# Two batches taken jointly through three parallel matrices by seven half products, with other conversion steps and first loads ahead of a branch

## The chip, the cores and the metric

The kernel runs on one core of one Trainium2 chip. A core has five engines that matter here: TensorE (PE, the matrix products; PEld are its weight loads), VectorE (DVE), ScalarE (ACT), GpSimd (POOL) and SyncE (SP), which issues most DMAs. The metric is the time of one execution on the device, in microseconds (us); less is better. A kernel's time is the median over its runs.

## What is computed

Four batches of softcap attention (12 heads, 448 tokens, 64 wide) give 1792 tokens of 768 numbers. Two feed-forward parts follow, each token by itself:

```python
x = softcap_attention(q, k, v, cap)             # 4 x 448 tokens, 768 wide
h = x @ w_in                                    # 768 -> 2048
g = where(h >= 1, h, where(h <= -1, 0, (h + 1)**2 / 4))
x = g @ w_out                                   # 2048 -> 768
h = maximum(maximum(x @ w1, x @ w2), x @ w3)    # three parallel matrices, 768 -> 768
out = h @ w_out2                                # the last matrix, 768 -> 768
```

The weights are float64 in memory, everything else is fp32.

## The kernel before

**Layout and products.** Activations lie transposed, so a tile is 128 features by the 448 tokens of one batch. A product of a 128x128 piece of a weight with such a tile is called a **part**: both factors are divided into a high and a low half (hi, lo; type fp32r), and a part is three matmuls of 128x448, hi with hi, hi with lo and lo with hi (`parts`, L863, L864, L865). For one batch w_in takes 16 x 6 = 96 parts, w_out 96, the three parallel matrices (W123) 108, the last matrix (W2) 36.

**Conversion.** There are 64 weight units: 16 of w_in (128x768), 24 of w_out (128x512), 18 of W123 and 6 of W2 (128x768). `fetch_first` (L385) loads a unit's 64-bit words and makes fp32 of them in steps: `s0` (L405, on ACT at L408 or on DVE) scales the low word to a few bits, `sign` (L414, DVE, L415) copies the sign bit, `s1` (L420, ACT, L422) rescales the high word, `s3` (L424, DVE, L426) puts them together in a tile named wf; the result is stored in DRAM (`scratch`). For later batches `fetch_again` loads it from there. `weights` (L454) divides wf into its halves w: hi by a copy on ACT (L276) or DVE (L278), lo by a subtraction on DVE (L281). In batch 1 the halves that the last stage uses are also stored (`parted`).

**Stages.** Batch 0's attention comes first (11 to 70 us). The first six units of w_in are then used in plain fp32 (`PLAIN`, one matmul L858 for a part). Then come batch 0's layers, with batch 1's attention between them (to about 320 us), batch 1's layers with the attention of batches 2 and 3 (to about 613 us), and `last_two` (from 625 us to the end): batches 2 and 3 jointly through all four layers by `strassen` (L1041), which makes a 2x2 block product from seven half products instead of eight (L1263). There a stage is one half product for a group of three blocks, in six banks of PSUM; the four weight sums (tiles ss) and the operand sums (tiles op) come from DVE, and what PE leaves in a bank is taken out and added by ACT or DVE (`put`, `plus`, tiles named s, sc, sv, M, Y, O).

**Attention.** For a pair of heads: scores (ps_s, L578 or L589), tanh (L596, ACT), exp (L643, ACT), sums of the exponentials (`total`, ps_r, L672), their reciprocals and the product with v (ps_a, L798). For the reciprocals a row of sums rs (L728 on ACT, L730 on DVE) is turned over by DMAs: `gather` (L744, issued at L750 from ACT's queue, rs to rc) and `spread` (SP's queue). `ADDED` tells of each batch how many additions of exponential tiles DVE makes before PE sums the rest: with 3, PE has 8 short matmuls (112x224) for a pair; with 2, 16.

**Order.** Every operation is handed to the class `Plan` with a cost on each engine that may do it, a time at which it is wanted, and what it depends on. `Plan.run` places all of them in one fixed order for each engine and chooses the engine (ACT or DVE) of copies. Engines work their own lists in that order; a tile of a pool (u, h, w, wf, raw, and in PSUM s, a, m) is taken when its last user is done. Everything exists twice, in the two arms of a `tc.If` on the cap's bits; with the cap of 30 the second arm runs (keep_max False). The load of the cap's bits (L204) comes ahead of the branch, all other loads after it.

## Time and profile before

| | before |
|---|---|
| time, median of 3 runs | 996.36 us (995.25 to 998.95) |
| the profiled execution's own time | 995.53 us |
| its span in the trace | 993.7 us, so 1.83 us lie outside it |
| granted TensorE clock, mean over the span | 0.993 |
| busy: PE, DVE, ACT, POOL | 963.0, 748.0, 602.0, 0.2 us |

The busy times are those of the whole span: PE is busy 97% of it by the profile, with pipelined matmuls whose records overlap. So a window in which PE is shown as fully busy can still hold time in which it waited; what its instructions need is better taken from the pitch of a long run of them. The rows are in the section behind the change.

### The profile page before, as it was taken

The numbers are of one execution on the slowest core, as the hardware profiler recorded it, in microseconds if no ns is written. First come the engines' busy times: TensorE is split into PE (matmuls) and PEld (weight loads), VectorE is DVE, ScalarE is ACT, GpSimd is POOL, SyncE is SP. The second block draws the span as 40 slices with busy tenths as digits, with TensorE's granted clock in tenths as the row PEclk, the third lists the DMA queues.
The fourth block names the chain that finished last, engine by engine and source line by source line (L and its number), as shares of the span: only waits on it lengthen the run. The fifth ranks groups of instructions, "written<-read, shape, count | busy, mean of one in ns | idle before, by whom it ended". The sixth has DMA issues, their size and how long they took to land.

```text
span 993.7 us, 14604 instructions
## 1 busy us (share of the span) xinstructions
PE 963.0 (97%) x5356; PEld 769.6 (77%) x5356; DVE 748.0 (75%) x1205; ACT 602.0 (61%) x876; POOL 0.2 (0%) x4
## 2 busy tenths in 40 slices
PE   5799999999999999999999999999999999999998
PEld 1124777877868877777777778999999999999997
DVE  1679999998989677877655667676898767858782
ACT  4788999787888478754445555555764524232431
POOL 0000000000000000000000000000000000000000
PEclk9799999999999999999999999999999999999999
DMA  5448877898898878688898765572364347437243
GB/s 127 150 147 261 264 230 226 266 292 274 289 293 270 293 248 277 224 283 286 289 319 275 228 209 188 166 238 80 129 200 139 107 147 235 136 103 238 88 147 131
DMA packets 111533, 210.96 MB, mean 212 GB/s; under 512 B 13022, under 2 KB 71518, under 8 KB 111454
## 3 DMA queue, kind: packets, MB, share of 16 engines
q1 hardware_dynamic: 109930, 209.87, 66.3%
q8 instruction: 44, 0.72, 0.3%
q10 hardware_dynamic: 1524, 0.08, 0.1%
q14 instruction: 35, 0.29, 0.1%
HBM read 142.90 MB, written 66.93 MB: 211 GB/s over the span
## 4 chain that ended last, share of the span: by engine, by line
PE 77%; ACT 9%; DVE 7%; DMA 4%; issue 2%; ACTq 0%; SPq 0%; DVEq 0%
PE ps_m L1263 21%; PE ps_s L1263 11%; PE ps_m L863 9%; PE ps_m L865 8%; PE ps_m L864 8%; PE ps_a L798 6%; PE ps_a L1263 5%; PE ps_s L578 4%; ACT raw L408 3%; PE ps_m L858 3%; DVE raw L415 2%; ACT t L643 2%; ACT raw L422 1%; DVE wf L426 1%; PE ps_s L589 1%
## 5 line engine op out<-in xcount | busy, mean ns | idle before, releaser
L1263 PE MATMUL ps_m<-op,w 128*128 128x448 f32 x1008 | 212.2, 368 | 0.0
L1263 PEld LDWEIGHTS ps_m<-op,w 128*128 128x128 f32 x1008 | 189.2, 188 | 19.1
L281 DVE TENSOR_TENSOR w<-wf,w 128x768 fp32r<-128x768 f32 (+1 forms) x146 | 120.6, 828 | 9.8 <-ACT w L276 8.0
L596 ACT ACTIVATE t<-ps_s,qscale 112x896 f32<-112x896 f32 x96 | 92.5, 1002 | 45.8 <-PE ps_s L578 39.2
L1263 PE MATMUL ps_s<-op,w 128*128 128x448 f32 x522 | 112.2, 368 | 0.0
L1263 PEld LDWEIGHTS ps_s<-op,w 128*128 128x128 f32 x522 | 98.0, 188 | 9.9
L643 ACT ACTIVATE t<-t,cap_sb 112x896 f32<-112x896 f32 x96 | 96.0, 1039 | 4.8 <-DVE rs L730 3.0
L276 ACT ACTIVATE w<-wf 128x768 fp32r<-128x768 f32 (+1 forms) x86 | 64.4, 750 | 55.9 <-PE ps_m L865 34.3
L798 PE MATMUL ps_a<-t,v 112*32 112x448 f32 (+1 forms) x752 | 82.8, 564 | 3.0 <-DVE xf L281 1.5
L863 PE MATMUL ps_m<-y,w 128*128 128x448 f32 x216 | 80.6, 373 | 0.0
L865 PE MATMUL ps_m<-y,w 128*128 128x448 f32 x216 | 79.2, 367 | 0.8 <-DVE w L281 0.8
L864 PE MATMUL ps_m<-y,w 128*128 128x448 f32 x216 | 79.0, 366 | 0.0
L278 DVE CAST w<-wf 128x512 fp32r<-128x512 f32 (+1 forms) x60 | 29.5, 492 | 57.3 <-PE ps_m L865 44.2
L863 PE MATMUL ps_m<-g,w 128*128 128x448 f32 x192 | 71.8, 374 | 0.0
L865 PE MATMUL ps_m<-g,w 128*128 128x448 f32 x192 | 70.5, 367 | 1.4 <-DVE w L281 1.4
L864 PE MATMUL ps_m<-g,w 128*128 128x448 f32 x192 | 70.3, 366 | 0.0
L422 ACT ACTIVATE raw<-raw 128x768 f32<-128x768 f32 (+1 forms) x64 | 53.6, 839 | 27.5 <-DVE raw L415 22.9
L415 DVE TENSOR_SCALAR raw<-raw 128x768 uint16<-128x768 uint16 (+1 forms) x64 | 60.1, 938 | 11.8 <-ACT raw L408 10.8
L408 ACT ACTIVATE raw<-raw 128x768 uint16<-128x768 uint32 (+1 forms) x37 | 62.9, 1700 | 2.2 <-DMA raw<-in_w_out 1.0
L281 DVE TENSOR_TENSOR w<-ss,w 128x384 fp32r<-128x384 f32 x80 | 43.7, 555 | 24.9 <-ACT w L276 22.8
L798 PEld LDWEIGHTS ps_a<-t,v 112*32 112x32 f32 (+1 forms) x752 | 24.2, 114 | 48.6 <-issue 32.8
L276 ACT ACTIVATE w<-ss 128x384 fp32r<-128x384 f32 x69 | 35.3, 520 | 40.8 <-PE ps_m L1263 21.0
(140 smaller groups left out, 1730.4 us busy)
## 6 DMA issues: line engine op xcount, KB each, us to landing
p<-w SPq DMA_DIRECT2D x60, 384.0 KB
w<-p SPq DMA_DIRECT2D x60, 384.0 KB
w<-wf SPq DMA_DIRECT2D x40, 384.0 KB
wf<-w SPq DMA_DIRECT2D x40, 384.0 KB
wf<-w SPq DMA_DIRECT2D x80, 192.0 KB
raw<-in_w SPq DMA_DIRECT2D x18, 768.0 KB
raw<-in_w_in SPq DMA_DIRECT2D x16, 768.0 KB
raw<-in_w_out SPq DMA_DIRECT2D x24, 512.0 KB
```

Of the source, the lines that this page charges most:

```text
L276: nc.scalar.activation(out=out_, in_=in_, func=AF.Copy)
L281: nc.vector.tensor_tensor(out=out_, in0=a, in1=b, op=o)
L408: nc.scalar.activation(out=out_, in_=lo, func=AF.Copy, scale=7.49 * 2.0**-32)
L415: nc.vector.tensor_scalar(out=part(U16, 1), in0=part(U16, 3), scalar1=0x8000, scalar2=None, op0=ALU.bitwise_and,)
L422: nc.scalar.activation(out=hi, in_=hi, func=AF.Copy, scale=2.0**-112)
L596: nc.scalar.activation(out=t[c].tile, in_=ps.tile[:C, :, :S], func=AF.Tanh, scale=qscale[:C])
L643: lambda e, c=c: nc.scalar.activation(out=t[c].tile, in_=t[c].tile, func=AF.Exp, scale=cap_sb[:C]),
L798: nc.tensor.matmul(pa.tile[j * D + d : j * D + d + n, :S], vt.tile[:, j, c, d : d + n], t[c].tile[:, j], start=start, stop=stop,)
L863: nc.tensor.matmul(ps.tile[:, :S], wh, a.tile[:, 0], start=start, stop=False)
L864: nc.tensor.matmul(ps.tile[:, :S], wh, a.tile[:, 1], start=False, stop=False)
L865: nc.tensor.matmul(ps.tile[:, :S], wl, a.tile[:, 0], start=False, stop=stop)
L1263: nc.tensor.matmul(get(), w_, x_, start=start and z == 0, stop=stop and z == 2, skip_group_check=begun,)
```

## The change

**Joint stage.** Batches 0 and 1 each go through w_in and w_out alone, as before. Their results are kept (`Y01`), and a new `first_two_end` takes both jointly: W123 by `strassen`, and then W2 in plain parts, each weight half serving both batches. W123 takes 9 blocks of 7 stages, with one block in a group: a stage is 3 parts, in one of two banks of the pool m that alternate (`two_banks`); each block's weights come from scratch, are summed and divided on chip (`new_blocks`) and their halves stored for `last_two` (`halves`). The order of the seven products is another one (`STAGES`), in `last_two` too.

**Conversion.** The 24 units of W123 and W2 are converted while batch 1 runs its layers, the other 40 before, as they were. `s0` writes 32-bit words in place of 16-bit ones, `sign` is a 32-bit scalar_tensor_tensor on both words, and `s1` may go to DVE.

**Rest.** The first heads' load, the cap's load and the constants stand ahead of the branch. The gather of the sums is issued from POOL's queue. `ADDED` is (3, 2, 2, 3). The relu reads PSUM directly instead of a copied tile. The attention results of batches 2 and 3 go to DRAM and come back for `last_two`. There the plain pieces of w_in and w_out, of which stored halves were loaded before, are loaded as fp32 and divided again (`divide_loaded`); the sums of w_out (`store_sums`) are made in the joint stage instead of batch 1's. Pools: u 37 to 35, wf 4 to 5.

```diff
+    bits = nc.values_load(cap.bitcast(I32)[0:1, 0:1])
+    const = ctx.enter_context(tc.tile_pool(name="const", bufs=1))
+    qk0 = const.tile([128, 2, qk.shape[4]], F32, name="qk0")
+    load_heads(nc, qk0, qk, 0, 0)
...
+    consts = const, qk0, cap_sb, ones, qscale
     with tc.If((bits & 0x7FFFFFFF) > LIMIT_BITS) as test:
-        softcap_attention_two_ffn(tc, qk, v, cap, *rest, keep_max=True)
+        softcap_attention_two_ffn(tc, consts, qk, v, *rest, keep_max=True)
     with test.Else():
-        softcap_attention_two_ffn(tc, qk, v, cap, *rest, keep_max=False)
...
-    ADDED, FOURS, POOLED = (3, 2, 3, 3), (0, 1, 2, 3), ()
+    ADDED, FOURS, POOLED = (3, 2, 2, 3), (0, 1, 2, 3), ()
...
-    slots = {"u": 37, "h": 9, "v": 3, "w": 4, "wf": 4, "raw": 3, "rc": 2, "s": 2, "a": 1, "m": 3}
+    slots = {"u": 35, "h": 9, "v": 3, "w": 4, "wf": 5, "raw": 3, "rc": 2, "s": 2, "a": 1, "m": 3}
...
-    PAIR0, LEAD0 = 9.0, 14.0
+    PAIR0, LEAD0 = 8.2, 8.0
...
-            lo, out_ = words()[0].bitcast(U32), part(U16, 0)
+            lo = words()[0]
             if e == "A":
-                nc.scalar.activation(out=out_, in_=lo, func=AF.Copy, scale=7.49 * 2.0**-32)
+                nc.scalar.activation(
+                    out=lo, in_=lo.bitcast(U32), func=AF.Copy, scale=7.49 * 2.0**-32
+                )
                 return
             nc.vector.tensor_scalar(
-                out=out_, in0=lo, scalar1=2.0**-29, scalar2=7.0, op0=ALU.mult, op1=ALU.min
+                out=lo, in0=lo.bitcast(U32), scalar1=2.0**-29, scalar2=7.0,
+                op0=ALU.mult, op1=ALU.min,
             )
 
         def sign(e):
-            nc.vector.tensor_scalar(
-                out=part(U16, 1), in0=part(U16, 3), scalar1=0x8000, scalar2=None,
-                op0=ALU.bitwise_and,
+            lo, hi = words()
+            nc.vector.scalar_tensor_tensor(
+                out=lo, in0=hi, scalar=-(2**31), in1=lo, op0=ALU.bitwise_and,
+                op1=ALU.bitwise_or,
             )
 
         def s1(e):
             hi = words()[1].bitcast(F32)
-            nc.scalar.activation(out=hi, in_=hi, func=AF.Copy, scale=2.0**-112)
+            if e == "A":
+                nc.scalar.activation(out=hi, in_=hi, func=AF.Copy, scale=2.0**-112)
+                return
+            nc.vector.tensor_scalar(
+                out=hi, in0=hi, scalar1=2.0**-112, scalar2=None, op0=ALU.mult
+            )
...
-                (nc.sync if pooled else nc.scalar).dma_start(out=rc.tile, in_=src)
+                queue = nc.sync if pooled else nc.scalar if keep_max else nc.gpsimd
+                queue.dma_start(out=rc.tile, in_=src)
...
+        r = op(
+            {"A": 0.57, "D": 0.62 if sb is ps else 0.4}, relu, w + (0.1 if sb is ps else 0.6), deps,
+            [sb], [u],
+        )
...
-                ys[m] = split("y", ps, done, w)
-        tops, ms = [half("top") for _ in range(NM)], [None] * NM
-        prevs = [None] * NM
-        if pair:
-            order = [(m + H2 * i, k) for m in range(H2) for k in range(3) for i in range(2)]
-        else:
-            order = [(m, k) for m in range(NM) for k in range(3)]
-        for m, k in order:
-            top = tops[m]
...
-        for m in half_and_half(NM):
...
+            y = Y01[m]
+            YA[m].append(op(
+                {"A": 0.53, "D": 0.62},
+                lambda e, y=y, ps=ps: copy(e, y.tile[:, b], ps.tile[:, :S]),
+                w, done, [ps, y], [] if b else [y],
+            ))
...
-    STAGES = ("A11", "A12", "S2", "S1", "S3", "S4", "A22")
-    BANK = (0, 1, 0, 0, 1, 0, 1)
-
-    def strassen(layer, pos, swap, blocks, groups, land):
+    STAGES = ("A11", "A12", "S2", "S3", "S1", "A22", "S4")
...
+    def two_banks(n):
+        A, B = ([buf("m", "ps_m", [P, 512]) for _ in range(n)] for _ in range(2))
+        def bank(x, i):
+            b_ = (A, B)[x][i]
+            return b_, (lambda: b_.tile[:, :S])
+        return bank
...
+        wa, da = both(whole(wf1), 2 * n, [wf1], [g1], starts[0] - 8)
+        keep_divided(u1, wa, da, starts[0])
+        wb, db = both(whole(ss[0]), 2 * n, [ss[0]], [o2, o3], starts[2] - 7)
+        wc, dc = both(whole(ss[1]), 2 * n, [ss[1]], [o1, o4], starts[4] - 7)
+        wd = buf("w", "w", [P, 2, WU], F32R)
...
+        where = [
+            (wa, 0, da), (wa, n, da), (wb, 0, db), (wb, n, db), (wc, 0, dc), (wd, n, [hi, lo]),
+            (wc, n, dc),
+        ]
+        return lambda stage, i, r, w: where[stage]
...
+                if at[0][0] not in halves:
+                    homes = [scratch[u][:, o : o + n] for u, o in at]
+                    return divide_loaded(wt, homes, [stored[u] for u, _ in at], w)
...
+        for n, u in enumerate(range(W1, NU)):
+            u = u if u >= W2 else W1 + (n // 6 + H2 * (n % 2)) * 3 + n % 6 // 2
+            fetch_first(u, begins(1) + 8 + n * (begins(2) - begins(1) + LATE) / (NU - W1))
+        for n in range(2 * H2):
+            store_sums(1, n % H2, n // H2, base + SUMS0 + SUMS1 * n)
+        M = [unit(f"M{m}") for m in range(NM)]
+        mdone = [[None, None] for _ in range(NM)]
+        base = strassen(
+            2, base, False, list(zip(Y01, YA)), [[x] for x in range(N2[2])],
+            largest(M, mdone, False), new_blocks, two_banks,
+        )
...
+        for m in range(NM):
+            u = W2 + m
+            wf, got = fetch_again(u, base)
+            w = divided(u, wf, got, base)
+            if m < H2:
+                keep_divided(u, *w, base)
+            else:
+                keep_divided(u, *w, base, KH)
+            for j in range(2):
+                ps, g = buf("m", "ps_m", [P, 512]), Group(NP)
+                done = parts(
+                    0, lambda q: base + q * PART, (*w, False), [x[j] for x in ms], 0, NP, ps, g,
+                    True,
+                )
+                for o in done[1:]:
...
-    last_two()
+    last_two(first_two_end(begins(2)))
```

**What moves in the engines' lists, SP's start.** The first rows of SP before; `qk<-in_qk` is the load of a pair of heads, `in_cap` the load of the cap's bits that the branch tests, and `v<-in_v` the values:

```order
L1488 UNCONDITIONAL_BRANCH
L204 TENSOR_LOAD in_cap_ptr
L204 TENSOR_LOAD in_cap
L205 REGISTER_ALU
L205 COMPARE_AND_BRANCH
L546 DMA qk<-in_qk 64x2x448 x2
L549 DMA v<-in_v 112x2x256
```

And after:

```order
L1607 UNCONDITIONAL_BRANCH
L239 DMA qk_65<-in_qk 64x2x448 x2
L211 TENSOR_LOAD in_cap_ptr
L211 TENSOR_LOAD in_cap
L228 REGISTER_ALU
L228 COMPARE_AND_BRANCH
L581 DMA v<-in_v 112x2x256
```

The first pair's load stood behind the test of the cap and stands ahead of it now.

**ACT in batch 0's attention.** Before, at the second and third gather; t are the tiles of scores (tanh L596, exp L643), rc<-rs the gather:

```order
L596 ACTIVATE t<-ps_s,qscale 112x896
L750 DMA rc<-rs 56x1x16
L643 ACTIVATE t<-t,cap_sb 112x896 x2
L596 ACTIVATE t<-ps_s,qscale 112x896
L643 ACTIVATE t<-t,cap_sb 112x896
L596 ACTIVATE t<-ps_s,qscale 112x896 x2
L643 ACTIVATE t<-t,cap_sb 112x896 x2
L750 DMA rc<-rs 56x1x16
L422 ACTIVATE raw<-raw 128x768
```

The same place after, where tanh is L631, exp L678, and L763 makes a row of sums rs:

```order
L631 ACTIVATE t<-ps_s,qscale 112x896
L678 ACTIVATE t<-t,cap_sb 112x896 x2
L631 ACTIVATE t<-ps_s,qscale 112x896
L678 ACTIVATE t<-t,cap_sb 112x896
L631 ACTIVATE t<-ps_s,qscale 112x896
L678 ACTIVATE t<-t,cap_sb 112x896
L308 ACTIVATE qk_hi<-qk 128x896
L763 ACTIVATE rs<-ps_r,eps_sb 128x224
L429 ACTIVATE raw<-raw 128x768
```

No DMA stands among ACT's rows there any more; the gathers are 23 rows on POOL.

**PE in the three parallel matrices.** Before, a block of one batch (y are the halves of its input, w those of the weight):

```order
L863 MATMUL ps_m_15125<-y_13788,w_15027 128x448
L864 MATMUL ps_m_15125<-y_13788,w_15027 128x448
L865 MATMUL ps_m_15125<-y_13788,w_15027 128x448
L863 MATMUL ps_m_15125<-y_14040,w_15027 128x448
L864 MATMUL ps_m_15125<-y_14040,w_15027 128x448
L865 MATMUL ps_m_15125<-y_14040,w_15027 128x448
```

And after, in a block of the joint stage (op are the operand sums or their halves; a row with x3 is a part):

```order
L1115 MATMUL ps_m_14320<-op_14036,w_14228 128x448 x3
L1115 MATMUL ps_m_14320<-op_14055,w_14228 128x448 x3
L1115 MATMUL ps_m_14320<-op_14061,w_14228 128x448 x3
L1115 MATMUL ps_m_14275<-op_14075,w_14285 128x448 x3
L1115 MATMUL ps_m_14275<-op_14111,w_14285 128x448 x3
L1115 MATMUL ps_m_14275<-op_14213,w_14285 128x448 x3
L1115 MATMUL ps_m_14320<-op_14083,w_14285 128x448 x3
L1115 MATMUL ps_m_14320<-op_14170,w_14285 128x448 x3
L1115 MATMUL ps_m_14320<-op_14222,w_14285 128x448 x3
L1115 MATMUL ps_m_14275<-op_14088,w_14304 128x448 x3
```

A bank was left alone for the six parts of a block, and now changes every three parts; the third stage adds into the bank of the first again.

**DVE at the same place.** After, the rows around the eviction of a stage (w are lo halves and sums of weights, ss weight sums, sv, s and M what is taken out of the banks):

```order
L313 TENSOR_TENSOR w_14372<-ss_14338,w_14372 128x768
L313 TENSOR_TENSOR sv_14380<-ps_m_14275,sv_14380 128x448
L313 TENSOR_TENSOR M3_14206<-sv_14380,M3_14206 128x448
L313 TENSOR_TENSOR ss_14401<-wf_14331,wf_14200 128x512
L313 TENSOR_TENSOR s_14294<-ps_m_14320,s_14294 128x448
```

The rows that empty a bank stand between the divisions and sums of the next blocks' weights, in one list.

## Rows read from the trace of the kernel before

**Rows 1.** Busy time by stretch: range, length, PE, PEld, DVE, ACT, POOL, clock, DMA share, GB/s

```profile
11.00:70.00 59.00, 50.56 (x401) 13.02 (x402) 34.79 (x50) 46.89 (x50) 0.00 (x0) 0.88 0.53 147
112.70:319.60 206.90, 199.83 (x1148) 161.51 (x1143) 191.84 (x281) 176.35 (x215) 0.00 (x0) 1.00 0.86 266
319.60:613.06 293.46, 293.46 (x1816) 231.81 (x1812) 204.05 (x307) 173.91 (x236) 0.00 (x0) 1.00 0.79 261
624.80:728.90 104.10, 104.10 (x505) 94.58 (x504) 77.44 (x149) 68.09 (x133) 0.00 (x0) 1.00 0.48 153
729.00:744.00 15.00, 15.00 (x74) 13.64 (x73) 14.06 (x26) 7.53 (x16) 0.00 (x0) 1.00 0.60 190
```

**Rows 2.** Chain that ended last: start, us, engine, output, line, count

```profile
81.00 22.75 PE ps_m L858 x60
...
382.32 3.01 PE ps_a L798 x32
385.33 1.41 PE ps_s L578 x12
...
729.10 14.88 PE ps_m L1263 x72
```

**Rows 3.** Windows of Rows 1 for line L863 alone: PE, PEld, clock, DMA share, GB/s

```profile
112.70:319.60 206.90, 97.47 (x261) 49.00 (x261) 1.00 0.86 266
319.60:613.06 293.46, 129.90 (x348) 65.33 (x348) 1.00 0.79 261
```

**Rows 4.** Timeline of PE at 238 us: start, us, line, operation, tiles, shape, count

```profile
238.70 0.96 PE L672 MATMUL ps_r<-se,ones 112*32 112x224 f32 x16
239.48 3.19 PE L798 MATMUL ps_a<-t,v 112*32 112x448 f32 x32
```

**Rows 5.** Chain, its start

```profile
0.72 0.86 SPq L204
...
2.24 2.53 issue
...
4.77 6.23 DMA qk<-in_qk
```

**Rows 6.** Waits of 11 to 78 us: who, for whom, us, times, longest

```profile
ACT raw L422 <- DVE rs L730: 3.7, 1, 3.7
...
ACT t L643 <- DVE rs L730: 3.0, 2, 2.2
```

**Rows 7.** Timeline of ACT's queue in the same stretch

```profile
46.42 0.53 ACTq L750 DMA_DIRECT2D rc<-rs  x1
```

**Rows 8.** Chain at 35 us

```profile
35.12 5.15 DMA rc<-rs
```

**Rows 9.** Groups by line and form: count | busy us, mean ns | idle before, releaser

```profile
L281 DVE TENSOR_TENSOR w<-wf,w 128x768 fp32r<-128x768 f32 x74 | 70.8, 958 | 3.8 <-ACT w L276 3.0 <-DMA p<-w 0.3
...
L415 DVE TENSOR_SCALAR raw<-raw 128x768 uint16<-128x768 uint16 x40 | 41.9, 1048 | 7.5 <-ACT raw L408 7.0
...
L408 ACT ACTIVATE raw<-raw 128x768 uint16<-128x768 uint32 x21 | 41.1, 1955 | 1.1 <-ACT rs L728 0.6 <-DMA raw<-in_w 0.5
...
L426 DVE SCALAR_TENSOR_TENSOR wf<-raw 128x768 int32<-128x768 int32 x40 | 38.4, 963 | 1.5 <-ACT raw L422 1.5
...
L422 ACT ACTIVATE raw<-raw 128x768 f32<-128x768 f32 x40 | 37.2, 932 | 20.5 <-DVE raw L415 16.6 <-DVE rs L730 3.7
...
L278 DVE CAST w<-wf 128x768 fp32r<-128x768 f32 x29 | 16.3, 561 | 26.2 <-PE ps_m L865 26.0
```

**Rows 10.** Timeline of DVE at 842 us, an eviction in the last stage

```profile
842.60 0.62 DVE L281 TENSOR_TENSOR sc<-ps_s,s 128x448 f32<-128x448 f32 x1 [0.17 <-PE ps_s L1263]
```

**Rows 11.** Waits over the whole span, one of ACT's

```profile
ACT w L276 <- PE ps_m L1263: 24.8, 26, 1.4
```

More of the change, by code (lines that the diff above doesn't have):

```diff
@@ L536, in attention @@
         vt = buf("v", "v", [C, 2, NCH, D])
-        qkt = [unit("qk")]
+        early = first and i == 0
+        qkt = [plan.fixed(qk0) if early else unit("qk")]
         t = [unit("t", rows=C) for _ in range(NCH)]
```

714 lines of the change are left out of this document (380 added, 334 removed).

## The prediction, made before the changed kernel ran

> **What bounds the kernel now.** I read the busy times by stage first [rows 1], then the chain that ended last [rows 2], then each stage's waits. PE is the bound nearly everywhere: batch 1's layers (319.60 to 613.06 us) show it busy for the whole window, the last stage too, and the chain runs through PE with only short pieces of other engines. But busy is not the same as needed. In a long undisturbed run 72 matmuls of 128x448 took 14.88 us [rows 2], so one costs 0.2067 us and a part of three 0.62 us. Against that price two stages have slack:
>
> - Batch 0's layers: the window of 206.90 us holds 3 x 261 = 783 layer matmuls (L863, L864 and L865 alike) [rows 3], 161.8 us. Five pairs of batch 1's attention add each the sums, 0.78 us (the product's start less the sums' start [rows 4]), the product with v, 3.01, and scores, 2 x 1.41 [rows 2], so 6.61 us a pair, 33.1. Left over: 206.9 - 161.8 - 33.1 = 12.0 us in which PE waited. DVE is busy for 191.84 and ACT for 176.35 of the 206.9 [rows 1]: this stage runs at the pace of the weight conversion.
> - Batch 1's layers: 3 x 348 = 1044 matmuls [rows 3] are 215.8 us; twelve pairs, with half as many sums, so 6.61 - 0.39 = 6.22 us, are 74.6; left over 293.46 - 290.4 = 3.0 us. Here PE's work itself is the bound, and DVE has 204.05 of 293.46 [rows 1].
>
> Batch 0's attention (11 to 70 us) is bound by neither: PE at a mean clock of 0.88, ACT busy for 46.89 of 59.00 [rows 1], and ACT stands twice behind a DMA issue of its own that waits for DVE's row of sums [rows 6].
>
> **The change part by part**, against the profiled run: span 993.7 us, 995.53 with what lies outside it (1.83), and 0.83 under the median of 996.36.
>
> 1. *PE's work.* Two batches took 2 x 108 x 3 = 648 matmuls through the three matrices; nine blocks of seven products of three parts take 9 x 7 x 3 x 3 = 567. So 81 fall away: 81 x 0.2067 = -16.7 us, all on PE, which is the path. Against it ADDED for batch 2 doubles the short sums of six pairs: 48 records more at 0.78/16 = 0.049 [rows 4], +2.3. Sum **-14.4**. This term is surest, since it is instructions that are not there. The last matrix keeps its matmuls; it only divides its weights once instead of twice.
>
> 2. *First loads ahead of the branch.* SP tests the cap, waits 2.53 us, issues the first pair at 4.77, and the data land 6.23 us later; PE starts at 11.05 [rows 5]. The load now goes out first, at about 0.72 us, so up to 4.05 us sooner. SP itself was past the branch at 4.77 us, so I take the other engines to be past theirs when the data land at about 7. ACT's first tanh needs constants made from the cap behind their own load; if these come only 2 us sooner, -2 is the other end. I take **-4**, since the cap's load moves up as well.
>
> 3. *Batch 0's attention.* The gather leaves ACT's queue. ACT stood 3.7 us once and 3.0 us in two waits behind it [rows 6], and issued five gathers at 0.53 us [rows 7], 2.7 us; 9.4 in all. Other waits (for PE, in which ACT would stand anyway) take part of that over: the exponentials need PE's scores, and these need a bank that ACT empties. I take half, **-5**; the range is -8 (nearly all) to +2 (the gather is issued later on POOL than it was on ACT, see the rivals). DVE's work in the window changes little.
>
> 4. *Conversion in batch 0's layers.* On ACT a unit's first step wrote 16-bit words and took 1.955 us, the next, 32-bit, 0.932 [rows 9]. A 32-bit first step has the second's form, so I take 0.93: -1.0 us for each unit of 768 columns for which it stays on ACT, 21 before. On DVE the 16-bit step on strided words took 1.048 and the sign copy the same; the sign step is now of the form of L426, 0.963 [rows 9], so nearly nothing changes there. Also 24 of 58 units leave for batch 1's stage, but the matmuls of W123 and W2 leave this stage with them, so DVE's load relative to PE's falls little: DVE's list from batch 0's first relu to batch 1's has 225 instructions, 171 us as a sum of their forms' means and some 156 with the overlap that records show now (0.91), against about 164 us of PE. That is 0.95; it was 192 of 200, or 0.96. So the 12.0 us of slack shrink, with the stage, and don't vanish. **-6**, half of it; bounds -12 and 0.
>
>  The Trainium skill ("VectorE: DVE Perf Modes", section "Mode 2×_2P — use both read ports for one tensor") says that an operation with one source in SBUF and 32-bit numbers can make two results per cycle. The cast of 768 columns at 561 ns beside subtractions of as many at 958 [rows 9] agrees with it. By it the 32-bit first and third step on DVE would come to about 0.56 us instead of 1.05, and this term would be nearer to -9.
>
> 5. *Batch 1's layers* take in the conversion of 24 units: two ACT steps and two DVE steps each, some 24 x (2 x 0.93) and 24 x (2 x 0.96) [rows 9], 45 us on each engine, less what falls away with W123 there. DVE's share rises from 0.70 to about 0.88 of PE's time, ACT's from 0.59 to about 0.80. A share of 0.9 is what batch 0's layers have, with 6% of slack, so some of it appears here: **+2**, bounds -1 (the 3.0 us of now get less) and +6 (2% to 3% of a stage of some 194 us).
>
> 6. *The joint stage.* A stage of one block is 9 matmuls, 9 x 0.2067 = 1.86 us, and then its bank must be emptied before the next but one stage starts in it. An eviction took 0.62 us and started 0.04 us after PE's end [rows 10], when DVE was free. With one instruction of 0.96 ahead in its list [rows 9]: 0.96 + 0.62 + 0.08 = 1.66, under 1.86, so it fits. In some of the 63 stages two stand in front. DVE is loaded to about 87% here by the same count. **+4** for all 63; bounds 0 and +15.
>
> 7. *`last_two`.* The plain pieces of w_in and w_out are divided again on chip: 12 more divisions for each layer, 24 x 0.958 [rows 9] = 23 us on DVE, where it had 77.44 of 104.10 us in the first layer [rows 1]. There it fits. Where the second layer's sums are divided, DVE already has 14.06 of 15.00 us and PE still has its full pitch [rows 1, 2]. **+2**, bounds 0 and +8.
>
> 8. At nothing: the relu that reads PSUM (one copy less on ACT or DVE, both beside PE), the attention results to DRAM and back (DMA is at 0.48 to 0.86 [rows 1], and the loads are issued long ahead), the pools.
>
> Sum: -14.4 - 4 - 5 - 6 + 2 + 4 + 2 = -21.4. Span 972.3, with 1.83 outside **974.1 us**.
>
> **The rivals.**
>
> - *Slower: the emptying of the banks sets the pace of the joint stage.* With two instructions ahead, 2 x 0.96 + 0.62 = 2.54 us passes the 1.86 by 0.7 us. ACT can stand too: its weight copy waited up to 1.4 us for one of the four w tiles [rows 11], and what it should empty stands behind that. If every one of 63 stages loses 0.7 us, this is +44 instead of +4: 1014. It turns slower than before from (995.5 - 974.1 + 4)/63 = 0.40 us per stage. For it: a bank changes six times as often as in the last stage, and DVE's list has the next block's weight work between the evictions. Against it: with one instruction ahead the eviction still fits, 1.66 of 1.86 us, and half of the evictions may go to ACT.
> - *The conversion stays the bound.* No gain in batch 0's layers (+6), +6 in batch 1's (+4 on the sum) and +8 in the joint stage (+4): 988. For it: DVE's load relative to PE's falls only from 0.96 to 0.95.
> - *The gather comes late on POOL.* The row of sums took 5.15 us through its DMA [rows 8]; if half of it, 2.6 us, is added in four rounds of batch 0's attention: +10, 984. The profile of now has nothing on POOL's queue, so nothing speaks against it. The Trainium skill ("SBUF — State Buffer", section "SBUF: two separate sides") says that a DMA of GpSimd's queue has descriptors written by software, which a DVE operation in a two-port mode locks out: about 620 ns alone and 3100 ns beside DVE copies. By that each round would lose some 2.5 us; no run shown here has such a DMA.
> - *All slack is filled*: -8 in the attention, -12 in batch 0's layers, -1 in batch 1's, 0 in the joint stage and the last: 993.7 - 14.4 - 4 - 8 - 12 - 1 = 954.3, with 1.83 956; I write 957.
> - *The gain is given back*: conversion and gather both, 974 + 14 + 10 = 998, no change.
>
> **How the numbers follow.** The forecast as it stands, within 8 us, 0.50; all slack filled 0.15; conversion 0.13; gather late 0.10; given back 0.06; slower by the banks 0.06. The predicted time is the likeliest's, 974. The range takes in everything from the filled slack to a little beyond the conversion case, 957 to 990; what is left out is the two last cases and a part of the tails, less than 2 in 10. About 0.5%, 5 us, is what a measurement of this kernel can tell from no change: under 991.4 is faster, 0.88 (the first four); between 991.4 and 1001.3 the same, 0.06; above it slower, 0.06.
>
> **What would show it.** In the profile after: 81 matmuls of 128x448 fewer and the same pitch of 0.2067 in undisturbed runs (step 1); first matmul at about 7 us (2); batch 0's attention 5 us shorter, no wait of ACT behind rs (3), and no growth of rc<-rs beyond 5.15; the first ACT step of the conversion near 0.93 us (4); PE's waits in batch 0's layers about 6 us (4), in batch 1's about 5 (5); in the joint stage 63 x 1.86 = 117 us plus no more than 4 (6). It would be wrong if PE waits in the joint stage for ps_m's release at most stages, if the slack of the first layers only moves to batch 1's, or if the 32-bit steps take longer than their rows.

## The result

| | before | after |
|---|---|---|
| time, median | 995.81 us (993.15 to 998.95, 4 runs) | 961.74 us (961.14 to 963.77, 4 runs) |
| ratio | | 0.966 (95% interval 0.9628 to 0.9692) |
| profiled execution, its span | 995.53, 993.7 us | 961.39, 959.6 us |

The kernel became 3.4% faster, 34 us. The prediction was 974 with a range of 957 to 990; so the time lies inside, 12 us below the likeliest value.

To see where the 34.1 us of span went, I set against each stage of both traces what its matmuls need: a layer matmul 0.2027 us (the faster of two paces, below), scores 0.110 (in fp32r 0.117), the product with v 0.098, short sums 0.049, a plain matmul 0.376 us, each by its usual start-to-start time in both traces. What a stage took beyond that is listed as "over": waits, switches between kinds of matmul, and a slower pace. Each trace is one execution.

| stage | before: us, over | after: us, over | change of over | forecast |
|---|---|---|---|---|
| to PE's first matmul | 11.05 | 7.66 | -3.4 | -4 |
| batch 0's attention | 58.80, 19.2 | 60.48, 18.8 | -0.5 | -5 |
| first plain units | 33.40, 2.5 | 37.70, 2.3 | -0.2 | |
| batch 0's layers | 235.52, 15.5 | 128.69, 3.0 | -12.5 | -6 |
| batch 1's layers | 286.03, 5.7 | 203.35, 8.2 | +2.5 | +2 |
| joint stage and last matrix | | 159.59, 0.9 | +0.9 | +4 |
| last stage | 368.96, 11.4 | 362.13, 4.6 | -6.8 | +2 |
| work at these prices, all stages | 928.3 | 914.2 | -14.1 | -14.4 |

The stages of after, as [rows 1] shows those of before (range, length, PE, PEld, DVE, ACT, POOL, clock, DMA share, GB/s): batch 0's layers, the joint stage, the last stage.

```profile
105.85:234.54 128.69, 128.69 (x807) 102.32 (x806) 111.42 (x179) 100.13 (x150) 3.03 (x5) 1.00 0.82 251
437.89:553.70 115.81, 115.32 (x568) 106.34 (x567) 102.15 (x169) 46.05 (x74) 0.00 (x0) 1.00 0.72 245
597.48:959.60 362.12, 358.20 (x1765) 331.01 (x1763) 283.68 (x523) 184.79 (x362) 0.00 (x0) 1.00 0.43 131
```

And one of before, batch 0's layers from their first fp32r matmul to the last:

```profile
103.24:338.75 235.51, 228.44 (x1310) 185.02 (x1309) 215.54 (x312) 193.80 (x239) 0.00 (x0) 1.00 0.86 269
```

DVE's busy share in batch 0's layers went from 0.92 to 0.87, ACT's from 0.82 to 0.78. The joint stage has 567 matmuls in 115.81 us, 0.2043 us each: nearly nothing of it is waiting, though DVE is busy for 0.88 of it.

Batch 0's layers of before fall into two parts, w_in with w_out, in which 33 units are put together in wf, and W123 with W2, in which 23 are:

```profile
103.24:226.80 123.56, 120.03 (x686) 96.66 (x685) 115.26 (x183) 108.91 (x148) 0.00 (x0) 1.00 0.85 258
226.80:338.75 111.95, 108.41 (x625) 88.36 (x624) 100.28 (x130) 84.90 (x92) 0.00 (x0) 1.00 0.88 282
```

At the prices of the table the first part is over by 8.5 us and the second by 7.0. The matmuls of the second part stand in the joint stage and its last matrix now, which are over by 0.9.

The start, from the chain of after (start, us, what); it answers to [rows 5]:

```profile
0.74 3.46 DMA qk<-in_qk
4.19 3.47 issue
7.66 3.31 PE ps_s L624 x12
```

The load lands at 4.2 us now. What PE waits for behind it is its own passage through the branch, until 7.66.

The conversion steps of after by form (count, busy us, mean ns, idle before), answering to [rows 9]: first step on ACT and on DVE, sign, third step on DVE.

```profile
L410 ACT ACTIVATE raw<-raw 128x768 int32<-128x768 uint32 x26 | 23.8, 914 | 0.1
L414 DVE TENSOR_SCALAR raw<-raw 128x768 int32<-128x768 uint32 x14 | 8.2, 586 | 0.5 <-DMA raw<-in_w 0.5
L421 DVE SCALAR_TENSOR_TENSOR raw<-raw 128x768 int32<-128x768 int32 x40 | 38.8, 969 | 1.1 <-ACT raw L410 0.6
L431 DVE TENSOR_SCALAR raw<-raw 128x768 f32<-128x768 f32 x22 | 12.4, 562 | 0.1
```

And the first step on DVE before, which [rows 9] leaves out:

```profile
L410 DVE TENSOR_SCALAR raw<-raw 128x768 uint16<-128x768 uint32 x19 | 19.9, 1046 | 0.3 <-DMA raw<-in_w_in 0.3
```

ACT's first step fell from 1955 to 914 ns, as forecast from the row of its 32-bit neighbour. DVE's first step fell from 1046 to 586 ns, where I had expected nearly no change. The third step, which only ACT did before, takes 562 ns on DVE. The sign step took 1048 ns before [rows 9] and takes 969 now.

Last, 72 matmuls in a row in the last stage, the piece of the chain that answers to [rows 2]:

```profile
728.97 14.60 PE ps_m L1115 x72
```

14.60 instead of 14.88 us, with the same granted clock of 1.00. This is small for one piece, but in these two traces it holds for all 1764 matmuls of the stage: 7.0 us.

### The profile page after: what moved, and what is told of

The parts are those of the page before. It is cut to its first block, busy times and chain, and to the rows that moved or that the text cites. A ratio compares the mean times of both kernels' runs of the same rounds, so it can differ in the third digit from the quotient of the medians.

```text
span 959.6 us, 14758 instructions
## 1 busy us (share of the span) xinstructions
PE 939.0 (98%) x5323; PEld 755.9 (79%) x5323; DVE 776.7 (81%) x1285; ACT 597.2 (62%) x935; POOL 14.5 (2%) x27
## 4 chain that ended last, share of the span: by engine, by line
PE 91%; issue 4%; DMA 2%; DVE 2%; ACT 1%; POOL 0%; POOLq 0%; DVEq 0%; ACTq 0%
PE ps_m L1115 32%; PE ps_s L1115 11%; PE ps_m L897 10%; PE ps_m L899 9%; PE ps_m L898 9%; PE ps_a L834 6%; PE ps_s L613 5%; PE ps_a L1115 5%; PE ps_m L892 3%; PE ps_r L707 1%; DMA rc<-rs 1%; DVE op L313 1%; PE ps_s L624 1%; DMA rc<-rc 0%; DMA qk<-in_qk 0%
## 5 line engine op out<-in xcount | busy, mean ns | idle before, releaser
L1115 PE MATMUL ps_m<-op,w 128*128 128x448 f32 x1575 | 324.1, 365 | 0.5 <-DVE M L313 0.5
L1115 PEld LDWEIGHTS ps_m<-op,w 128*128 128x128 f32 x1575 | 295.6, 188 | 24.5 <-DVE M L313 0.9
L313 DVE TENSOR_TENSOR w<-wf,w 128x512 fp32r<-128x512 f32 (+2 forms) x155 | 117.3, 760 | 13.7 <-ACT w L308 11.4
L308 ACT ACTIVATE w<-wf 128x512 fp32r<-128x512 f32 (+2 forms) x124 | 84.2, 682 | 63.8 <-PE ps_m L1115 30.7
L631 ACT ACTIVATE t<-ps_s,qscale 112x896 f32<-112x896 f32 x96 | 92.7, 1004 | 32.1 <-PE ps_s L613 22.5
L678 ACT ACTIVATE t<-t,cap_sb 112x896 f32<-112x896 f32 x96 | 96.4, 1040 | 0.3
L308 ACT ACTIVATE w<-ss 128x384 fp32r<-128x384 f32 (+1 forms) x93 | 53.1, 583 | 64.9 <-PE ps_m L1115 37.4
L313 DVE TENSOR_TENSOR w<-ss,w 128x384 fp32r<-128x384 f32 (+1 forms) x98 | 59.7, 626 | 14.4 <-ACT w L308 14.0
L437 DVE SCALAR_TENSOR_TENSOR wf<-raw 128x768 int32<-128x768 int32 (+1 forms) x64 | 55.0, 860 | 5.7 <-ACT raw L429 4.6
L421 DVE SCALAR_TENSOR_TENSOR raw<-raw 128x768 int32<-128x768 int32 (+1 forms) x64 | 55.2, 863 | 4.8 <-ACT raw L410 4.1
L897 PE MATMUL ps_m<-x,w 128*128 128x448 f32 x156 | 58.7, 376 | 0.0
L899 PE MATMUL ps_m<-x,w 128*128 128x448 f32 x156 | 57.0, 366 | 0.0
L898 PE MATMUL ps_m<-x,w 128*128 128x448 f32 x156 | 57.0, 365 | 0.0
L1115 PE MATMUL ps_a<-op,w 128*128 128x448 f32 x234 | 51.3, 365 | 0.0
```

Of the source, the lines that this page charges most:

```text
L308: nc.scalar.activation(out=out_, in_=in_, func=AF.Copy)
L313: nc.vector.tensor_tensor(out=out_, in0=a, in1=b, op=o)
L421: nc.vector.scalar_tensor_tensor(out=lo, in0=hi, scalar=-(2**31), in1=lo, op0=ALU.bitwise_and, op1=ALU.bitwise_or,)
L437: nc.vector.scalar_tensor_tensor(out=wf.tile[:, :n].bitcast(I32), in0=hi, scalar=3, in1=lo, op0=ALU.logical_shift_left, op1=ALU.bitwise_or,)
L631: nc.scalar.activation(out=t[c].tile, in_=ps.tile[:C, :, :S], func=AF.Tanh, scale=qscale[:C])
L678: lambda e, c=c: nc.scalar.activation(out=t[c].tile, in_=t[c].tile, func=AF.Exp, scale=cap_sb[:C]),
```

## The experiments

All are made from the changed kernel, except one from the kernel before. "Over" is the quantity of the table above.

**1. Seven half products undone (no_halves).** `strassen` of the joint stage replaced by plain parts for both batches with one weight load; the conversion's order follows that of the units.

```diff
-        base = strassen(
-            2, base, False, list(zip(Y01, YA)), [[x] for x in range(N2[2])],
-            largest(M, mdone, False), new_blocks, two_banks,
-        )
+        for m in range(NM):
+            for k in range(3):
+                u = W1 + 3 * m + k
+                wf, got = fetch_again(u, base)
+                w = divided(u, wf, got, base)
...
+                for j in range(2):
+                    ps, g = buf("m", "ps_m", [P, 512]), Group(NP)
+                    done = parts(
+                        0, lambda q: base + q * PART, (*w, False), [x[j] for x in ys], 0, NP, ps,
+                        g, True,
+                    )
```

> The changed kernel, with the three parallel matrices of batches 0 and 1 as eight products in plain parts (one weight load and division for both batches) in place of the seven half products: 648 matmuls instead of 567. Theory (the joint stage gives what its matmuls are and costs almost nothing): 81 x 0.2027 = +16.4 us, less the 0.8 us that PE waited in the joint stage, 977. Rival (the sums, divisions and evictions of the half products press on DVE beyond the stage, so that part of the gain is paid back elsewhere): +8 to +13, 970 to 975.

Measured: 976.14 us (974.43 to 979.37), ratio to before 0.9818 (0.9784 to 0.9851). From batch 1's layers to the end of the last matrix, by stretch, first this kernel and then the changed one:

```profile
231.59:610.78 379.19, 378.97 (x2258) 305.97 (x2256) 263.38 (x405) 194.27 (x267) 7.50 (x12) 1.00 0.78 253
```

```profile
234.54:597.48 362.94, 362.45 (x2177) 290.66 (x2175) 306.87 (x480) 228.74 (x323) 7.50 (x12) 1.00 0.80 257
```

81 matmuls more and 16.25 us longer: 0.2006 us for each. The theory holds. The half products cost DVE 43 us more work here and PE gets all of its gain. Without the half products the kernel still beats the one before by 20 us, so the rest of the change gives over half of the 34 us.

**2. The first load behind the branch again (late_load).**

```diff
-    load_heads(nc, qk0, qk, 0, 0)
...
-        ql = None if early else op(
+        ql = op(
...
-            begin - (10 if full else 6), takes=qkt,
+            begin - (10 if full else 6), takes=[] if early else qkt,
```

> The changed kernel with the first pair's load back behind the branch (the cap's load and the constants stay ahead of it). Theory (the load ahead of the branch is worth what PE starts sooner, 11.05 to 7.66 us): first matmul at 10.4 to 11.1 us, and all behind it later by as much, +3 us, 965. Rival (the attention behind it is bound by rounds and exponentials that start by the clock of other loads): first matmul late, but the end only 0 to 1 us later.

Measured: 965.81 us (965.03 to 966.18), 0.9696 (0.9677 to 0.9715). The chain of this kernel:

```profile
5.72 5.32 DMA qk<-in_qk
...
11.09 3.38 PE ps_s L623 x6
```

PE starts 3.4 us later and the end comes 4.1 later. The theory holds; nothing behind it takes the time up.

**3. The gather on ACT's queue again (gather_act).**

```diff
-                queue = nc.sync if pooled else nc.scalar if keep_max else nc.gpsimd
+                queue = nc.sync if pooled else nc.scalar
...
-            r = op({"Q": 0.1} if pooled else {"A": 0.6} if keep_max else {"P": 1.0}, gather, w + 0.05, [ep], [src], [rc])
+            r = op({"Q": 0.1} if pooled else {"A": 0.6}, gather, w + 0.05, [ep], [src], [rc])
```

> The changed kernel with the gather of the row of sums issued from ACT's queue again. Forecast's theory (leaving ACT's queue was worth 5 us in batch 0's attention): 961.7 + 5 = 967. Rival, read from the two traces (the round of the sums through DMAs sets that stretch, and its first two rounds grew from 4.94 and 5.66 to 6.72 and 7.68 us from sums to reciprocals with the gather on POOL): the rounds shorten by 1.5 to 2 us each and the time falls by 2 to 5 us, 957 to 960. Third (the other DMA traffic, not the queue, made the rounds longer): rounds of 6 to 7 us stay, ACT waits again, 962 to 966.

Measured: 960.98 us (958.01 to 965.94), 0.9672 (0.9631 to 0.9714): no difference from the changed kernel that this can tell. ACT's wait behind the gather does not return as it was [rows 6]:

```profile
ACT t L678 <- DVE rs L765: 1.1, 1, 1.1
```

So 1.1 us and not 6.7: the order of the work around the gather is another one now, and the gather's queue alone was not what ACT lost. From sums to reciprocals the five rounds took 5.4 to 6.4 us bar one of 4.7, from POOL 4.7 to 7.7; their means are 5.6 and 6.0, and batch 0's attention is over by 16.4 here and 18.8 there, in one trace each. The loss of 5 us that the forecast's theory asks for isn't seen, and 967 lies above all four runs; between the two others the run doesn't decide.

**4. The 16-bit conversion steps again (conv16).**

```diff
-            lo = words()[0]
+            lo, out_ = words()[0].bitcast(U32), part(U16, 0)
...
-            nc.vector.scalar_tensor_tensor(
-                out=lo, in0=hi, scalar=-(2**31), in1=lo, op0=ALU.bitwise_and,
-                op1=ALU.bitwise_or,
+            nc.vector.tensor_scalar(
+                out=part(U16, 1), in0=part(U16, 3), scalar1=0x8000, scalar2=None,
+                op0=ALU.bitwise_and,
```

The third step was left as in the changed kernel, free to go to DVE.

> The changed kernel with the 16-bit conversion steps of before (first step on ACT 1.96 us for 768 columns, sign copy on words of 16 bits, third step on ACT alone). Theory (the 32-bit steps took away most of the 12.5 us that PE waited in batch 0's layers): PE's waits there return for the most part, +6 to +12 us, 968 to 974, and some in batch 1's layers where 24 units are converted. Rival (the waits went because the 24 units of W123 and W2 left that stage): 0 to +2 us, 962 to 964.

Measured: 966.01 us (960.85 to 973.37), 0.9721 (0.966 to 0.9783). The runs scatter widely. In its trace batch 0's layers are as free of waits as in the changed kernel:

```profile
107.22:235.39 128.17, 128.17 (x807) 102.20 (x806) 113.44 (x177) 113.05 (x151) 3.19 (x5) 1.00 0.80 249
```

ACT has 13 us more to do there and PE loses nothing (over 2.5 against 3.0). What the trace does show longer lies elsewhere: 2.9 us in the plain units, which are the first to want converted weights, and 1.6 in batch 1's layers. The second is no more than other kernels here differ by (8.4 to 9.6 us over in seven others with the new steps and the same ADDED, 9.8 here). By the medians the cheaper steps are worth some 4 us, but the intervals of the two ratios overlap, so their worth isn't shown. They are not why the waits of batch 0's layers went: the theory falls.

**5. The relu from a copied tile again (relu_copy).**

```diff
-            s = square_relu(lambda h=h: h.tile, h, done, w, ps)
+            a = op(
+                {"A": 0.53, "D": 0.62}, lambda e, h=h, ps=ps: copy(e, h.tile, ps.tile[:, :S]),
+                w, done, [ps], [h],
+            )
+            s = square_relu(lambda h=h: h.tile, h, [a], w)
```

> The changed kernel with the relu reading a copied tile again, as before: one copy of 128x448 more for each of 32 blocks of batches 0 and 1, 0.53 to 0.62 us each on ACT or DVE. Theory (the waits of batch 0's layers went because W123 and W2 with their conversions left the stage): PE waits in that stage stay under 4 us as in the changed kernel, 0 to +2 us in all, 961 to 964. Rival (the copy that fell away on the path from a block's product to the next layer is what emptied the stage): PE's waits in it rise to 8 or more, 968 and up.

Measured: 964.01 us (962.15 to 968.39), 0.9674 (0.9653 to 0.9695). Batch 0's layers are over by 3.4 us instead of 3.0, batch 1's by 9.5 instead of 8.2. The rest of its profiled execution's extra time is the pace of matmuls, which is slow here from 452 to 826 us (run 10). The rival falls.

**6. The 24 units converted in batch 0's layers again (conv_b0).**

```diff
-            fetch_first(u, begins(1) + 8 + n * (begins(2) - begins(1) + LATE) / (NU - W1))
+            fetch_first(u, begins(0) + 8 + n * (begins(1) - begins(0) + LATE) / (NU - W1))
```

> The changed kernel with the 24 units of W123 and W2 converted during batch 0's layers, as before, instead of batch 1's. In the changed kernel DVE is busy for 111.4 of the 128.7 us of batch 0's layers and ACT for 100.1. Theory (conversion beside PE is the resource of this stage, and putting 24 units elsewhere is what took the waits away): each unit brings about 1.9 us on DVE and 1.8 us on ACT, 24 x 1.9 = 46 us on DVE where 17 were free; PE waits 20 to 35 us there, some of it won back in batch 1's layers: 975 to 995. Rival (the stage has room, since the steps are cheaper now): 962 to 967.

Measured: 1021.36 us (1017.92 to 1026.67), 1.0256 (1.0209 to 1.0302): slower than the kernel before. Batch 0's layers by stretch, and the two largest waits of PE between 105 and 270 us:

```profile
108.87:298.01 189.14, 152.41 (x806) 110.27 (x805) 162.13 (x245) 119.55 (x168) 3.02 (x5) 0.90 0.91 292
```

```profile
PE ps_m L897 <- ACT w L308: 12.3, 8, 2.9
PE ps_m L899 <- DVE w L313: 7.9, 13, 1.0
```

60 us longer for the same matmuls, twice what I had expected; PE is idle for 36.7 us of the stage and waits for divided weights. DVE is busy for 0.86 of the stage, hardly other than in the changed kernel (0.87), so it isn't simply full; DMA has 0.91 and 292 GB/s, the highest of all stages here, and PE's granted clock falls to 0.90 in the mean. Which of these sets the 60 us is open. That the place of these 24 conversions decides about the stage is shown: 51 units beside 468 layer matmuls are too many, 31 are not. The run does not bring the stage of before back, though: there 56 units stood beside 900 layer matmuls, since W123 and W2 were in it. So it shows that the conversions had to leave once these matmuls had left, and not that their leaving took the waits of before away.

**7. Three additions for batch 2 again (added3), and two for batch 3 as well (added2).**

```diff
-    ADDED, FOURS, POOLED = (3, 2, 2, 3), (0, 1, 2, 3), ()
+    ADDED, FOURS, POOLED = (3, 2, 3, 3), (0, 1, 2, 3), ()
```

> The changed kernel with three additions of exponential tiles on DVE for each pair of batch 2, as before: 48 short matmuls fewer on PE, and six additions of 112x896 (1.1 us) more on DVE in batch 1's layers, where DVE is busy for 176.0 of 203.4 us. Theory by the price of the sums (0.049 us each): -2.3 us, 959 to 960. Rival (conversion and attention together press DVE there, so six more additions of 1.1 us in its list delay PE): 0 to +5, 962 to 967.

Measured: 967.46 us (963.14 to 969.15), 0.97 (0.9668 to 0.9732), so about 6 us slower, not 2.3 faster. Batch 1's layers by stretch, and what PE waits for in them:

```profile
236.13:445.65 209.52, 204.14 (x1346) 142.61 (x1344) 180.42 (x264) 170.89 (x223) 7.75 (x12) 0.99 0.83 253
```

```profile
PE ps_s L613 <- ACT t L631: 3.8, 4, 1.8
PE ps_a L834 <- DVE xf L313: 1.0, 1, 1.0
```

48 short matmuls fewer, and the stage is 6.2 us longer (209.52 for 203.35): over rises from 8.2 to 16.7. In the changed kernel PE waits for none of these there. The order of the work in this stage shifts with the edit, so the six additions are the occasion, not each one's price.

```diff
-    ADDED, FOURS, POOLED = (3, 2, 2, 3), (0, 1, 2, 3), ()
+    ADDED, FOURS, POOLED = (3, 2, 2, 2), (0, 1, 2, 3), ()
```

> The changed kernel with two additions of exponential tiles on DVE for each pair of batch 3 as well. With three for batch 2 (the run before) PE's waits in batch 1's layers grew from 8.2 to 16.7 us for 2.35 us less of sums. Theory (each six additions on DVE cost PE 6 us net there): -2 to -4, 958 to 960. Rival (that stage's remaining waits have other causes, and PE's own 48 records count in full): +2.35, 963 to 965.

Measured: 961.2 us (957.99 to 969.6), 0.9684 (0.9637 to 0.9731): the same as the changed kernel. Over falls from 8.2 to 6.8, which pays for half of the 2.35 us of sums. As far as this run tells, what could be had was had with batch 2.

**8. Every eviction of the joint stage on DVE (evict_dve).**

```diff
-        return {"A": 0.53, "D": 0.62}
+        return {"A": 0.53, "D": 0.62} if not dve_only else {"D": 0.62}
...
+        dve_only.append(1)
         base = strassen(
             2, base, False, list(zip(Y01, YA)), [[x] for x in range(N2[2])],
             largest(M, mdone, False), new_blocks, two_banks,
         )
+        dve_only.clear()
```

> The changed kernel with every emptying of a bank in the joint stage placed on DVE; in the changed kernel 30 of the 63 were on ACT, where 16.3 us were spent on them and ACT was busy for only 46 of 115.8 us, and DVE was busy for 102.2. Theory of the slower rival (emptying the banks from one loaded list stalls PE): DVE has 102.2 + 30 x 0.62 = 120.8 us of work in a stage of 115.8, so +5 us at least, and with evictions behind weight work up to +20: 967 to 982. Against it (there is room, weight work can wait): 0 to +2, 962 to 964.

Measured: 968.79 us (966.92 to 969.81), 0.9727 (0.9708 to 0.9746). PE's waits in the joint stage:

```profile
PE ps_m L1115 <- DVE M L310: 1.8, 2, 1.4
PE ps_m L1115 <- DVE s L310: 1.2, 2, 0.8
```

The joint stage and the last matrix are over by 5.4 us instead of 0.9, some 0.6 of it by the slower pace; another 2.6 us of the profiled execution are the slower pace in part of the last stage. So the mechanism of the slower rival is there, as soon as DVE alone empties the banks: a few waits of up to 1.4 us, not 0.7 us in each of 63 stages. In the changed kernel ACT does 30 of the 63 and the stage is free of it.

**9. The first loads of weights later (late_raw20), and that with the gather on ACT (late_gather).**

```diff
-        a = op({"Q": 3.4 * k}, load, want - lead - 12, takes=[raw])
+        a = op({"Q": 3.4 * k}, load, want - lead - (12 if i >= PLAIN else -8), takes=[raw])
```

> The changed kernel with the loads of the first six weights wanted 20 us later, so that four instead of seven stand ahead of the last round of sums in batch 0's attention, as before the change. In the changed kernel the DMA share from 28 to 68 us is 0.69, before the change it was 0.38 from 30 to 70 us. Theory (this traffic lengthens the rounds of the sums, 6.72 and 7.68 us in the first two against 4.94 and 5.66, and hides ACT's gain): rounds of 5 to 6 us, attention 2 to 4 us shorter; the plain units that follow wait up to 2 us for their weights: 958 to 962. Rival (the rounds don't set that stretch, or early loads feed the next stage): attention the same, later stages 2 to 8 us longer, 963 to 970.

Measured: 957.35 us (954.38 to 958.28), 0.9608 (0.9586 to 0.9629): the fastest of all, 0.5% under the changed kernel; none of its runs reaches the changed kernel's lowest. The stretch from 28 to 68 us, first of the changed kernel and then of this one, and from 30 to 70 of before:

```profile
28.00:68.00 40.00, 32.58 (x256) 9.12 (x252) 31.62 (x45) 31.41 (x36) 2.42 (x4) 0.83 0.69 214
```

```profile
28.00:68.00 40.00, 34.24 (x267) 9.81 (x264) 31.82 (x46) 35.39 (x40) 2.42 (x4) 0.91 0.65 203
```

```profile
30.00:70.00 40.00, 32.90 (x269) 8.61 (x266) 28.90 (x41) 31.43 (x34) 0.00 (x0) 0.83 0.38 122
```

The rounds are 5.2 to 6.2 us, on average 5.6 instead of 6.0, and the longest of the changed kernel, 7.7, is gone. The attention is over by 14.9 instead of 18.8. But kernels whose attention is unchanged differ as much among themselves (15.2 in added2, 19.5 in added3), the DMA share fell only from 0.69 to 0.65, and the plain units are handled in another order too. The rounds don't account for it either: added2, whose attention was as short as here, had rounds of 6.0 us on average and one of 9.2. Nor had all rounds grown with the change, as the first two had: those of the kernel before average 5.5 us, and its third took 7.5. So the gain is measured by the runs' times, and that it comes from the traffic is not shown.

> The later first loads of late_raw20 together with the gather on ACT's queue of gather_act. In the traces from the issue of the gather to the reciprocal: 4.5 to 5.5 us from POOL and 4.2 to 5.9 from ACT, and the issue itself 0.6 us on POOL beside 0.53 on ACT. Theory (the traffic lengthened the rounds, the queue hardly matters): 956 to 959, as late_raw20 with 957.4. Rival (the gather on POOL costs the rounds something of its own, which the traffic covered): 951 to 955. Third (ACT's waits behind the gather are worth the 5 us that were forecast): 961 to 963.

Measured: 960.06 us (959.25 to 961.44), 0.9647 (0.9628 to 0.9665): 2.7 us over late_raw20, none of the three cases. 2.6 us of its profiled execution are the slower pace in a part of the last stage, but that execution is the fastest of this kernel and the profiled one of late_raw20 its slowest, so the traces don't explain the difference. The move to ACT's queue gained 0.8 us in run 3 and lost 2.7 here: as far as these runs tell, POOL's queue neither helps nor hurts much.

**10. Interruptions in the last stage of the kernel before (pace_before).**

```diff
+                                if stage == 0 and k == 0 and i == 0:
+                                    nc.tensor.matmul(
+                                        get()[:D, :D], ones, ones, start=True, stop=True
+                                    )
```

> The kernel before, with one small fp32 matmul (64x64 from the tile of ones, overwritten at once) ahead of the first part of each of the eight groups of the last stage. In the trace of before the 1764 matmuls of that stage start every 206.7 ns throughout, in the changed kernel every 202.7 ns; elsewhere both paces appear, and one changes into the other only where the run of matmuls is interrupted. Theory (the pace is a matter of how a run begins, and an interruption draws it anew): some groups fall to 202.7 ns; the stage gains up to 7 us less 1 to 2 us for the interruptions, 989 to 996. Rival (the pace belongs to the code or the banks of this stage in the kernel before): all groups stay at 206.7, +1 to +2 us, 997 to 998.

Measured: 993.89 us (988.76 to 996.35, 10 runs), 0.9971 (0.995 to 0.9991). The chain of this kernel at the second interruption, and 54 matmuls behind it; in the kernel before 54 matmuls took 11.16 us in this stage:

```profile
667.66 0.26 PE ps_m L1263 x2
...
679.07 10.94 PE ps_m L1267 x54
```

All eight groups run at 202.7 ns in this trace: the stage went from 368.96 to 365.20 us, with some 3.2 us paid for the interruptions. The rival falls: the slow pace belongs neither to the code nor to the banks. That the interruption draws the pace is less sure: only the first one follows matmuls at 206.7 ns (41 in a row), the other seven follow matmuls that had 202.7 already. And in relu_copy the changed kernel's own code ran at the slow pace until 826 us and at the fast one behind a wait there; 504 matmuls of the joint stage, and 54 later:

```profile
451.26 104.42 PE ps_m L1119 x504
...
842.64 10.94 PE ps_m L1119 x54
```

In the changed kernel the same 504 took less:

```profile
451.45 102.42 PE ps_m L1115 x504
```

## Why the prediction was right, and where its steps were off

- **What bounds the kernel**: right. PE is the path, and removing matmuls from it gives their full price: undoing the half products alone cost 16.25 us of 16.4. Step 1's -14.4 stands as -14.1 in the table because the same 81 matmuls are priced at the faster pace there; the measurement is the 16.25.
- **ADDED inside step 1**: mis-judged. As PE work it did cost 2.35 us. But I booked it as a cost alone; run 7 shows that it saved 8.5 us of waits in batch 1's layers and so about 6 net. Step 5's +2 was met (+2.5) only with it.
- **Step 2, the start**: -3.4 of -4. Its release is not the load (landed at 4.2) but PE's own passage through the branch, which I had taken to be earlier: its branch instruction (L228) takes 4.96 us and ends at 7.60. Why it takes so long isn't shown. In ten more kernels with the same loads ahead of the branch PE starts at 6.7 to 7.7 us.
- **Step 3, batch 0's attention**: the term of -5 failed as put, -0.5 in the profiled execution. ACT's waits behind rs are gone, as forecast, but the stage is no shorter for it: taking half of ACT's waits for time of the stage was the wrong step. Single traces of this stretch scatter: over 19.2 and 22.4 in two traces with the order of before, 15.2 to 19.5 in seven with the conversion and the queues of after, so the mean gain is some 3 us. That it comes from the gather's queue is not borne out (run 3). Seven loads of raw weights stand in that stretch before its last round instead of four, which I didn't see; asking for them later gave 4.4 us by the medians, on a path that stays open (run 9).
- **Step 4, batch 0's layers**: the term of -6 was mis-sized, -12.5. (At the 0.2067 us a matmul that I had counted with, it is -10.8, from 11.9 to 1.1, and inside its bounds.) I argued that conversion per PE time stays the same, and over the whole stage it did: 56 units beside 235.5 us and 31 beside 128.7, 0.24 per us. Yet the waits went from 6.6% to 2.3%. The trace of before splits the 12.5. 7.0 us of it left the stage with the matmuls of W123 and W2; the joint stage and the last matrix, where these stand now and which I had priced apart at +4, are over by only 0.9. The other 5.5 went in w_in and w_out themselves, from 8.5 to 3.0; there 33 conversions stood beside 123.6 us, 0.27 per us, and 31 stand beside 128.7 now, 0.24, since three more are done ahead of the stage and more of batch 1's attention is placed in it. So conversion per PE time did fall in this part. In late_raw20, where 33 stand beside 133.5 us, the stage is over by 3.2. Whether this ratio is the cause wasn't tested. Neither the 32-bit steps (run 4) nor the relu (run 5) by itself is the reason, and with these matmuls gone the 24 units had to leave as well (run 6). What else there is (a fifth wf tile, other due times of the loads) wasn't tried, so the rest of this term stays open. The Trainium skill's rule on one-source operations ("VectorE: DVE Perf Modes", "Mode 2×_2P — use both read ports for one tensor") is borne out by the trace: 586 and 562 ns, where I had named 0.56 us after the cast. The larger gain in this stage that I worked out from it is not: run 4 takes the first step's part of it back without a wait in the stage.
- **Step 6, the joint stage**: +0.9 instead of +4. One eviction per 1.86 us fits, because ACT takes half of them; the slower rival needs DVE alone, and even so costs 4.5 us more (run 8) where I had priced 44 in all.
- **Step 7, the last stage**: the 23 us of divisions on DVE cost 0.2 us of waits, where I took +2; and -7.0 came from a cause that no step had, the pace (run 10). This one term is over half of the 12 us that were missed. That the time still came out within the range is in part luck: the attention's missing 4.5 us was set off by more than its size in steps 4, 6 and 7.
- **The rival of the late gather**: in the trace POOL issued 23 gathers in 0.62 us each on average. Nearly all took 0.60 to 0.61; the longest, 0.85, is the only one in which a DVE operation with one source in SBUF began and ended:

```profile
318.40 0.85 POOL L786 DMA_DIRECT2D rc<-rs  x1 [15.21 <-DVE rs L765]
318.56 0.56 DVE L414 TENSOR_SCALAR raw<-raw 128x768 int32<-128x768 uint32 x1
```

The issue ends 0.14 us behind that operation. The Trainium skill's rule ("SBUF — State Buffer", "SBUF: two separate sides"), by which such a DMA takes about 3.1 us in place of 0.62 beside a DVE copy, agrees in kind and not in size: the delay is 0.25 us, once in 23 issues and not in batch 0's attention. The 2.6 us a round that I had given this rival aren't seen: the five rounds average 6.0 us, against 5.5 before.

## What to carry to other kernels

Where PE is the path, matmuls taken away give their start-to-start price in full, as they did here with what replaces them spread over two engines; so look who empties the banks. An edit that costs the bound engine a little and frees a loaded one can still win: price both engines, not only the bound one. And conversion work should be judged by the stage it stands in: the same 24 units were nearly free in one stage and cost 60 us in the one before. A stage's waits are best split by the matmuls they stand at before one asks which edit removed them: here more than half of them had left with their matmuls.

## What the runs showed of the hardware

- **Two paces of the same matmul.** At a granted clock of 1.00 (the level of 2.4 GHz), an unbroken run of 128x448 matmuls with a weight load for each starts every 202.7 ns or every 206.7 ns in the mean, and mostly stays at one of them (1805 in a row at 206.7 in the kernel before). It changes mostly where the run is broken by a wait or by other matmuls, but not only there: in the traces of the changed kernel (at 443.2 us), late_load (447.9) and pace_before (267.0) it changed with no more than 0.21 us between any two starts. It cost the kernel before 7.0 us in its last stage, and the profiled executions of relu_copy, evict_dve and late_gather 2.6 to 7 us. Behind all eight interruptions by a small matmul it was the faster one, but only one of them came behind matmuls at 206.7 ns; what decides it is open.
- **A conversion that writes strided 16-bit words from 32-bit ones** took 1955 ns for 768 columns on ACT, 914 when it writes 32-bit words; on DVE 1046 and 586.
- **A gather issued from POOL beside DVE.** Over the ten traces with the gather on POOL's queue (230 issues), an issue took 0.60 to 0.61 us bar each kernel's first (0.74) and 19 others of 0.61 to 1.36 us. Each of the 19 ended 0.14 us behind a DVE operation with one source in SBUF that ran beside it; the longest, in conv16, stood beside one of 1.07 us.
- **Batch 0's attention varies from execution to execution**: six kernels with the same order of work in it took between 56.9 and 61.2 us for it, one trace each. A change of 3 us there can't be read from one trace.
